# A two-layer MLP behind attention in fp32: the copies of layer one's output leave from another queue, and the order of late conversions changes

## The chip, the core and the metric

The kernel runs on one core of one Trainium2 chip. A core has five engines, each with an instruction queue of its own that is worked off in order: TensorE (matrix products; PE, its weight loads PEld), VectorE (DVE), ScalarE (ACT), GpSimd (POOL) and SyncE (SP), which here only starts DMA transfers. ScalarE can start transfers from its own queue too, in line with its arithmetic. The metric is the device time of one execution in microseconds; of several runs the median counts.

## The reference

Attention over 4 batches, 8 heads, 576 positions and 64 channels gives x, the sum of a local part (each query sees keys less than 4 positions away) and a part on means of 4 positions. Two gated layers follow; the last line is the output, 2304 x 512.

```python
x = np.ascontiguousarray(attn_out.transpose(0, 2, 1, 3)).reshape(B * S, H * D)   # 2304 x 512
h = x @ w_in                                 # layer one, 512 x 2048
x = (h * (1.0 / (1.0 + np.exp(-h)))) @ w_out # 2048 x 512
h = x @ w2_in                                # layer two
out = (h * np.clip(h + 3.0, 0.0, 6.0) / 6.0) @ w2_out
```

## The kernel before

**Numbers.** All products are made from fp32 operands split into a high and a low part of a faster format (hi and lo; `gh`, `gl`, `xhl`, `xa`, `xb`, `w`). Three products, hi by hi, lo by hi and hi by lo, are summed in PSUM. The weights arrive as words of twice the width, so each tile of a weight is converted once: `conv_parts` makes two halves of the number (`wu` on ScalarE, `wt` on GpSimd), `conv_join` puts them together in two operations on VectorE, `split_w` makes hi on ScalarE and lo on GpSimd. One conversion so costs two operations on each of the three.

**Layer one** goes over 8 units of 288 tokens, and in each unit over 16 tiles f of the inner width. For each f: 12 matmuls make h (`gemm1`), ScalarE takes the tanh (`t<-h`), VectorE makes the gate, ScalarE and VectorE or GpSimd split it (`gh`, `gl`), and two f later 12 matmuls add to the four accumulators y (`y_unit1`). The attention of the next unit is woven into these steps. At the end of a unit `end_unit1` (line 965) copies the four y out of PSUM on ScalarE (`yo`) and sends each copy to DRAM (`x2d`), 144 KB a piece; line 969 starts the transfer on ScalarE's queue. Units 0 to 2 are handled in passes of their own; from unit 2 to unit 6 the steps are held in program order (`strict`). Some weights of layer one don't stay in SBUF from unit 2 on: they lie ready in DRAM (`wsd`) and are loaded again each time by `swap_w` (`w<-wsd`), because their slots are used to prepare layer two.

**Preparing layer two.** The first product of layer two is made with seven instead of eight block products, on sums of quarter blocks of `w2_in` and of x. From unit 2 on the sums of the weights are made in small steps (`COMBO`), and `combo_store` (line 292) writes them to DRAM (`wcd`). `load_ring` (line 328) brings them back, 512 KB for each of three parts and 256 KB for the seventh, into 16 slots that layer one's weights free. In the last unit (7), `load_w` loads the 16 tiles of `w2_out` (`raw`, 512 KB each), each as soon as the layer-one tile in its slot is done with; `add_w` (line 1066) lists the 16 conversions, and `step()` runs one after each f from 7 on. `load_x2` loads the first 512 tokens of layer one's output, `sums_x2`, `split_x2a` and `split_x2b` make the sums of x.

**Layer two** goes over 4 blocks of 512 tokens and one of 256, each in 8 steps (`at`, 40 in all). A step makes the seven products (24 matmuls in `first_phase`, 18 in `second_phase`), the gate (`gates2`) and its split into g (two halves, `split_g2`), and adds the two products of the step before (`y_unit2`, 12 matmuls each). Step `at` uses the tiles p and p + 8 of `w2_out`, p counting 0 to 7 in the block.

**Order of the work.** The program text is written in the order in which the steps are meant to go, but a scheduler that simulates the timeline chooses the order of each engine's queue; `tc.issue_after` (in `behind`, `in_line`) pins an instruction behind another. Every transfer reports its end in one of eight counters, named DMAHW0 to DMAHW7 in the listings below; they are given out in turn to the transfers of both queues, and a transfer is started only when the one before it on its counter has ended.

## Time and profile before

| | us |
|---|---|
| median of 3 runs (948.66, 954.82, 953.62) | 953.62 |
| the profiled execution | 943.39 |
| its span, first to last instruction | 941.6 |
| TensorE busy in it | 907.6 |
| VectorE, ScalarE, GpSimd busy | 528.3, 414.1, 354.5 |

The profiled execution is 10.2 us (1.1%) below the median of the runs; 1.8 us of it lie outside the span. TensorE is busy in 96% of the span, so what is left to gain sits in the other 34 us, or in stretches where it runs at the lower of its two clock levels.

### The profile page before, as it was taken

The numbers are of one execution on the slowest core, as the hardware profiler recorded it, in microseconds if no ns is written. First come the engines' busy times: TensorE is split into PE (matmuls) and PEld (weight loads), VectorE is DVE, ScalarE is ACT, GpSimd is POOL, SyncE is SP. The second block draws the span as 40 slices with busy tenths as digits, with TensorE's granted clock in tenths as the row PEclk, the third lists the DMA queues.
The fourth block names the chain that finished last, engine by engine and source line by source line (L and its number), as shares of the span: only waits on it lengthen the run. The fifth ranks groups of instructions, "written<-read, shape, count | busy, mean of one in ns | idle before, by whom it ended". The sixth has DMA issues, their size and how long they took to land.

```text
span 941.6 us, 21071 instructions
## 1 busy us (share of the span) xinstructions
PE 907.6 (96%) x8231; PEld 836.0 (89%) x8231; DVE 528.3 (56%) x1050; ACT 414.1 (44%) x973; POOL 354.5 (38%) x456
## 2 busy tenths in 40 slices
PE   7889989999999799999999989999999999999998
PEld 5778988999999799999999978898888888898896
DVE  4977697266465356654634765556446544644422
ACT  5667546344353354453535443443235324422432
POOL 7568864225554244663345932142006002300100
PEclk9879999999999999999999989999999999999999
DMA  8949846226857648666469985558567655754570
GB/s 209 305 141 282 255 122 153 79 72 163 253 167 200 171 143 202 213 179 203 145 195 350 400 311 176 183 173 267 167 181 227 210 176 171 246 170 153 157 268 24
DMA packets 172908, 185.09 MB, mean 197 GB/s; under 512 B 90632, under 2 KB 140040, under 8 KB 172808
## 3 DMA queue, kind: packets, MB, share of 16 engines
q1 hardware_dynamic: 168200, 179.02, 62.5%
q10 hardware_dynamic: 4608, 4.72, 1.5%
q8 instruction: 65, 1.06, 0.5%
q14 instruction: 35, 0.29, 0.1%
HBM read 154.21 MB, written 29.49 MB: 195 GB/s over the span
## 4 chain that ended last, share of the span: by engine, by line
PE 75%; DMA 7%; DVE 6%; POOL 5%; ACT 3%; issue 3%; SPq 1%; ACTq 0%; DVEq 0%; POOLq 0%
PE y L348 36%; PE m L348 18%; PE h L348 16%; DMA vraw<-in_v_dram 2%; PE lv L348 1%; DVE wt L31 1%; POOL w L31 1%; DMA raw<-in_moe_w_out_dram 1%; POOL wt L31 1%; PE ls L348 1%; DVE t L31 1%; DMA raw<-in_moe_w_in_dram 1%; PE dv L348 1%; DMA qkraw<-in_q_dram 1%; PE dt L355 1%
## 5 line engine op out<-in xcount | busy, mean ns | idle before, releaser
L348 PE MATMUL y<-gh,w 128*128 128x288 f32 x1024 | 230.4, 301 | 12.3 <-ACT gh L31 6.2
L348 PE MATMUL h<-xhl,w 128*128 128x288 f32 x1536 | 232.7, 300 | 4.2 <-DVE t L31 2.4
L348 PEld LDWEIGHTS h<-xhl,w 128*128 128x128 f32 x1536 | 213.0, 191 | 10.9 <-DVE t L31 3.3
L348 PE MATMUL y<-w,g 128*128 128x512 f32 x864 | 216.2, 397 | 2.4 <-ACT g L31 1.2
L348 PEld LDWEIGHTS y<-w,g 128*128 128x128 f32 x864 | 157.0, 188 | 36.8 <-DVE g L31 2.8
L348 PEld LDWEIGHTS y<-gh,w 128*128 128x128 f32 x1024 | 173.6, 191 | 15.8 <-ACT gh L31 7.3
L31 DVE SCALAR_TENSOR_TENSOR t<-t,h 128x288 f32<-128x288 f32 (+1 forms) x192 | 100.7, 527 | 129.6 <-ACT t L31 129.3
L31 POOL TENSOR_TENSOR gl<-t,gh 128x288 fp32r<-128x288 f32 x112 | 94.6, 845 | 175.4 <-ACT gh L31 163.7
L348 PE MATMUL y<-gl,w 128*128 128x288 f32 x512 | 151.0, 300 | 0.7 <-DVE gl L31 0.6
L31 ACT CAST gh<-t 128x288 fp32r<-128x288 f32 x128 | 55.3, 432 | 102.3 <-PE y L348 55.1
L348 PEld LDWEIGHTS y<-gl,w 128*128 128x128 f32 x512 | 97.8, 191 | 2.4 <-DVE gl L31 1.7
L348 PEld LDWEIGHTS m<-xa,ring 128*128 128x128 f32 x720 | 91.8, 191 | 3.4
L348 PE MATMUL m<-xa,ring 128*128 128x256 f32 x720 | 93.4, 282 | 0.0
L31 POOL TENSOR_TENSOR w<-wt,w 128x512 fp32r<-128x512 f32 x48 | 63.2, 1320 | 71.5 <-ACT w L31 64.1
L31 ACT ACTIVATE t<-h 128x288 f32<-128x288 f32 x128 | 52.2, 408 | 85.4 <-PE h L348 73.6
L31 ACT ACTIVATE t<-m,three 128x256 f32<-128x256 f32 x48 | 22.8, 474 | 145.4 <-PE m L348 141.9
L31 DVE SCALAR_TENSOR_TENSOR t<-t,m 128x256 f32<-128x256 f32 x48 | 20.2, 421 | 115.3 <-ACT t L31 115.3
L348 PEld LDWEIGHTS m<-xb,ring 128*128 128x128 f32 x624 | 78.4, 188 | 3.4
L348 PE MATMUL m<-xb,ring 128*128 128x256 f32 x624 | 79.4, 279 | 0.0
L31 DVE SCALAR_TENSOR_TENSOR wt<-wu,wt 128x512 uint32<-128x512 uint32 x96 | 65.4, 685 | 18.7 <-POOL wt L31 11.4
L31 POOL TENSOR_TENSOR xa<-xsum,xa 128x512 fp32r<-128x512 f32 x9 | 12.4, 1385 | 139.4 <-ACT xa L31 139.4
L31 DVE TENSOR_TENSOR g<-t,g 128x512 fp32r<-128x512 f32 (+1 forms) x80 | 59.3, 748 | 9.7 <-ACT g L31 9.6
(94 smaller groups left out, 1056.2 us busy)
## 6 DMA issues: line engine op xcount, KB each, us to landing
ring<-wcd SPq DMA_DIRECT2D x120, 512.0 KB
w<-wsd SPq DMA_DIRECT2D x44, 512.0 KB
raw<-in_moe_w_out_dram SPq DMA_DIRECT2D x32, 512.0 KB
raw<-in_moe_w_in_dram SPq DMA_DIRECT2D x16, 512.0 KB
craw<-in_moe_w_in_dram SPq DMA_DIRECT2D x32, 256.0 KB
sevenths<-wcd SPq DMA_DIRECT2D x32, 256.0 KB
wcd<-chi SPq DMA_DIRECT2D x16, 384.0 KB
wcd<-comb SPq DMA_DIRECT2D x16, 384.0 KB
```

The costliest lines, as they stand in the source:

```text
L31: r = getattr(self.engine, name)(*args, **kwargs)
L348: latest[0] = nc.tensor.matmul(*args, **kwargs).ins
L355: latest[0] = nc.tensor.transpose(*args).ins
```

## The change

Five edits, in the order of the diff. `combo_store` writes one block of sums with two transfers instead of four, because `wcd` gets another layout: for each partition 4 rows of 896 words. `load_ring` then gathers four pieces of 1 KB per partition where it read one of 4 KB, and four of 512 B for the seventh where it read one of 2 KB. The copies of layer one's output (`x2d`) are started from SyncE's queue instead of ScalarE's. In the last unit the third group of ring tiles is no longer written into its program, and seven steps of conversion run instead of nine, in another order of the tiles; in the first block of layer two every step runs two, pinned behind what each engine was last given. And the sums of the next x are pinned in the same way.

```diff
@@ -104,7 +104,7 @@
     x0d = dpool.tile([P, NC, UT], F32, name="x0d")
     y0d = dpool.tile([NC, P, UT], F32, name="y0d")
     wsd = dpool.tile([2, NF, P, 2 * DM], U32, name="wsd")
-    wcd = dpool.tile([HP, P, 3584], U32, name="wcd")
+    wcd = dpool.tile([HP, P, 4, 896], U32, name="wcd")
 
     def setup():
         make_identity(nc, ident)
@@ -292,14 +292,7 @@
     def combo_store(i):
         j, ci = divmod(i, 2)
         for s, t in enumerate((cw["hi", i], cw["c", i])):
-            t = t.bitcast(U32)
-            at = s * 512 + ci * 256
-            nc.sync.dma_start(
-                wcd[j, :, 0:3072].rearrange("p (i w) -> p i w", i=3)[:, :, at:at + 256],
-                t[:, 0:6].rearrange("p (i k) f -> p i (k f)", k=2),
-            )
-            at = 3072 + s * 256 + ci * 128
-            nc.sync.dma_start(wcd[j, :, at:at + P], t[:, 6])
+            nc.sync.dma_start(wcd[j, :, 2 * s + ci], t.bitcast(U32)[:, 0:7].rearrange("p k f -> p (k f)"))
 
 
 
@@ -330,12 +323,14 @@
         src = wcd[q % HP]
         if i < 3:
             t = slot(0, RING[k][i], [P, 2, 2, 2, P], F32R, "ring")
-            nc.sync.dma_start(t.rearrange("p s c k f -> p (s c k f)").bitcast(U32), src[:, i * 1024:(i + 1) * 1024])
+            nc.sync.dma_start(
+                t.rearrange("p s c k f -> p (s c) (k f)").bitcast(U32), src[:, :, 256 * i:256 * (i + 1)]
+            )
         else:
             if k // 2 not in sevenths:
                 sevenths[k // 2] = slot(0, SEVENTHS[k // 2], [P, 2, 2, 2, 1, P], F32R, "sevenths")
             t = sevenths[k // 2][:, k % 2]
-            nc.sync.dma_start(t.rearrange("p s c k f -> p (s c k f)").bitcast(U32), src[:, 3072:3584])
+            nc.sync.dma_start(t.rearrange("p s c k f -> p (s c) (k f)").bitcast(U32), src[:, :, 768:896])
         ring[q, i] = t
 
     def combo(q, n):
@@ -966,7 +961,7 @@
         for m in range(NC):
             yo = pool.tile([P, UT], F32, tag="de" if m == 3 else "le" if u >= NU - 2 else "wt", name="yo", bufs=3)
             act.activation(yo, ys[m], AF.Copy, scale=0.5)
-            nc.scalar.dma_start(x2d[m, :, u * UT:(u + 1) * UT], yo)
+            nc.sync.dma_start(x2d[m, :, u * UT:(u + 1) * UT], yo)
 
     def end_half1(u, ys):
 
@@ -985,7 +980,7 @@
     def end_half2(u, ys):
         for m, yo in enumerate(y0s):
             vec.scalar_tensor_tensor(out=yo, in0=ys[m], scalar=0.5, in1=yo, op0=ALU.mult, op1=ALU.add)
-            nc.scalar.dma_start(x2d[m, :, u * UT:(u + 1) * UT], yo)
+            nc.sync.dma_start(x2d[m, :, u * UT:(u + 1) * UT], yo)
 
     def y_unit2(i, f, ys):
         step_until((1, 1, f))
@@ -1030,10 +1025,10 @@
 
 
     RINGED = {}
-    for n in range(3):
+    for n in range(2):
         for i in range(4):
             f = RING[n][i] if i < 3 else SEVENTHS[n // 2] if n % 2 == 0 else max(RING[n])
-            RINGED.setdefault(15 if n == 2 else f, []).append((n, i))
+            RINGED.setdefault(f, []).append((n, i))
 
     HF = NF // 2
     passes = [(0, range(HF)), (1, range(NF)), (0, range(HF, NF))] + [(u, range(NF)) for u in range(2, NU)]
@@ -1063,7 +1058,7 @@
             if n_pass < 2:
                 step_until((0, 0, f))
             if f == 3 and u == NU - 1:
-                add_w([(1, 1, i) for i in range(NF)])
+                add_w([(1, 1, i) for i in (0, 1, 2, 8, 3, 9, 10, 11, 4, 12, 5, 13, 6, 14, 7, 15)])
             strict[0] = n_pass > 2 and u < NU - 1
             with line():
                 h = gemm1(0, f, x, UT)
@@ -1126,7 +1121,7 @@
                     split_x2a(0)
                 if f == 12:
                     split_x2b(0)
-                if f >= 7:
+                if f >= 9:
                     step()
 
     strict[0] = False
@@ -1213,11 +1208,14 @@
             with in_line():
                 flush(0)
             load_w(1, 1, NF - 1)
-            for i in range(4):
-                load_ring(3, i)
+            for k4 in (2, 3):
+                for i in range(4):
+                    load_ring(k4, i)
             second_phase(u, 1, *first_two[0])
         if u == 0:
-            step()
+            for _ in range(2):
+                with behind(dict(last)):
+                    step()
         for i in (1, 0, 3, 2):
             if at + 4 < n_q and (i < 3 or at + 4 < n_q - HP):
                 load_ring(at + 4, i)
@@ -1232,7 +1230,8 @@
             if p < sizes[u + 1] // XC:
                 load_x2(u + 1, p)
             if p == 4:
-                sums_x2(u + 1)
+                with behind(dict(last)):
+                    sums_x2(u + 1)
         late = p, y2
     for i in range(2):
         y_unit2(i, late[0] + HP * i, late[1])
```

**At the end of a unit.** ScalarE's queue at the end of unit 3, before; `[waits ...]` names the counters of transfers (DMAHW) and of engines for which a row waits.

```order
L31 CAST gh<-t 128x288 [waits DVE_49]
L31 ACTIVATE t<-h 128x288 [waits PE_49,Pool_49]
L31 ACTIVATE yo<-y 128x288 [waits PE_49] x2
L969 DMA x2d<-yo 128x288 [waits DMAHW2_49,Activation_49]
L31 CAST gh<-t 128x288 [waits DVE_49,PE_49]
L969 DMA x2d<-yo 128x288 [waits DMAHW4_49,Activation_49]
L31 ACTIVATE yo<-y 128x288 x2
L31 ACTIVATE t<-h 128x288 [waits PE_49,Pool_49]
L969 DMA x2d<-yo 128x288 [waits DMAHW5_49,Activation_49]
```

SyncE's queue before, a little ahead of that in the program; its fourth row is a reload with the counter DMAHW2, for which the first copy above waits.

```order
L228 DMA w<-wsd 128x1024 [waits DMAHW7_49,PE_49]
L361 DMA qkraw<-in_k_dram 32x18x32 [waits DMAHW0_49]
L361 DMA qkraw<-in_k_dram 32x18x32 [waits DMAHW1_49]
L228 DMA w<-wsd 128x1024 [waits DMAHW2_49,PE_49]
L361 DMA qkraw<-in_q_dram 32x9x32 [waits DMAHW3_49,DVE_49]
L361 DMA qkraw<-in_q_dram 32x9x32 [waits DMAHW4_49]
```

The same place of ScalarE's queue in the changed kernel:

```order
L31 ACTIVATE t<-h 128x288 [waits PE_49,Pool_49]
L31 CAST gh<-t 128x288 [waits DVE_49]
L31 ACTIVATE t<-h 128x288 [waits PE_49,Pool_49]
L31 ACTIVATE yo<-y 128x288 [waits PE_49] x3
L31 CAST gh<-t 128x288 [waits DVE_49,PE_49]
L31 ACTIVATE yo<-y 128x288
L31 ACTIVATE t<-h 128x288 [waits PE_49,Pool_49]
L31 CAST gh<-t 128x288 [waits DVE_49,PE_49]
```

And SyncE's queue there, changed kernel: the four copies stand behind the loads of q and k, and ahead of the stores of sums and four reloads of weights.

```order
L228 DMA w<-wsd 128x1024
L356 DMA qkraw<-in_k_dram 32x18x32 x2
L228 DMA w<-wsd 128x1024
L356 DMA qkraw<-in_q_dram 32x9x32 x4
L356 DMA qkraw<-in_k_dram 32x18x32 x4
L964 DMA x2d<-yo 128x288 x4
L295 DMA wcd<-chi 128x896
L295 DMA wcd<-comb 128x896
L242 DMA craw<-in_moe_w_in_dram 128x2x256 x2
L228 DMA w<-wsd 128x1024 x4
```

What moved: no transfer is left between the tanh, the copies and the split on ScalarE; the copies' transfers stand on SyncE's queue in one piece.

**At the end of layer one.** ScalarE's queue before, from the tanh of f = 12 to the split of f = 14. The rows `t_7999`, `t_8050`, `t_8093` and `t_8144` are the tanh of f = 12, 13, 14 and 15; `wu_8074`, `wu_8117` and `wu_8180` are the first halves of the conversions of tiles 6, 7 and 8.

```order
L31 ACTIVATE t_7999<-h_7986 128x288 [waits PE_49]
L31 CAST gh_8002<-t_7999 128x288 [waits DVE_49,PE_49]
L31 ACTIVATE t_8050<-h_8037 128x288 [waits PE_49,Activation_49]
L31 CAST gh_8053<-t_8050 128x288 [waits DVE_49,PE_49]
L31 ACTIVATE wu_8074<-raw_7827 128x512 [waits DMAHW5_49]
L31 ACTIVATE wu_8117<-raw_7872 128x512 [waits DMAHW1_49]
L31 CAST w_8114<-wt_8076 128x512 [waits DVE_49,DMAHW2_49,Activation_49,Pool_49]
L31 ACTIVATE wu_8180<-raw_7921 128x512 [waits DMAHW4_49]
L31 ACTIVATE t_8093<-h_8080 128x288 [waits PE_49]
L31 CAST w_8177<-wt_8119 128x512 [waits DVE_49,Activation_49,Pool_49]
L31 ACTIVATE t_8144<-h_8123 128x288 [waits PE_49]
L31 CAST gh_8096<-t_8093 128x288 [waits DVE_49]
```

The changed kernel, from the split of f = 12 to the tanh of f = 15. Here `t_8000`, `t_8043` and `t_8086` are the tanh of f = 13, 14 and 15, and `wu_7981`, `wu_8024`, `wu_8067` belong to tiles 8, 3 and 9.

```order
L31 CAST gh_7952<-t_7949 128x288 [waits DVE_49,PE_49]
L31 ACTIVATE wu_7981<-raw_7871 128x512 [waits DMAHW3_49]
L31 ACTIVATE wu_8024<-raw_7676 128x512 [waits DMAHW5_49]
L31 CAST w_8021<-wt_7983 128x512 [waits DVE_49,Activation_49,Pool_49]
L31 ACTIVATE wu_8067<-raw_7925 128x512 [waits DMAHW5_49]
L31 ACTIVATE t_8000<-h_7987 128x288 [waits PE_49]
L31 CAST w_8064<-wt_8026 128x512 [waits DVE_49,Activation_49,Pool_49]
L31 ACTIVATE t_8043<-h_8030 128x288 [waits PE_49]
L31 CAST gh_8003<-t_8000 128x288 [waits DVE_49]
L31 CAST w_8119<-wt_8069 128x512 [waits DVE_49,Activation_49,Pool_49]
L31 CAST gh_8046<-t_8043 128x288 [waits DVE_49]
L31 ACTIVATE t_8086<-h_8073 128x288 [waits DVE_49,PE_49]
```

What moved: the three waits for transfers stood between the tanh of f = 13 and that of f = 14, and stand now between the split of f = 12 and the tanh of f = 13.

**In the first steps of layer two.** VectorE's queue in the step of the third pair, before, from the gate to the next copy from PSUM (`t2` and `h` are the gate, `g2` the two halves of g, `wt` the joining of a converted tile):

```order
L31 SCALAR_TENSOR_TENSOR t2_8187<-t2_8187,m_8409 128x256 [waits Activation_49]
L31 TENSOR_TENSOR h_8436<-m_8410,s_8435 128x512 [waits PE_49]
L31 SCALAR_TENSOR_TENSOR t2_8187<-t2_8187,h_8436 128x256 [waits Activation_49]
L31 SCALAR_TENSOR_TENSOR t2_8187<-t2_8187,h_8436 128x512 [waits Activation_49]
L31 SCALAR_TENSOR_TENSOR wt_8586<-wu_8584,wt_8586 128x512 [waits Activation_49,Pool_49]
L31 TENSOR_TENSOR g2_8186<-t2_8187,g2_8186 128x512 [waits Activation_49]
L31 SCALAR_TENSOR_TENSOR wt_8586<-wu_8584,wt_8586 128x512 [waits DVE_49]
L31 TENSOR_TENSOR g2_8186<-t2_8187,g2_8186 128x512 [waits Activation_49]
L31 TENSOR_TENSOR s_8536<-m_8510,s_8536 128x256 [waits Activation_49]
```

The same step in the changed kernel:

```order
L31 SCALAR_TENSOR_TENSOR t2_8129<-t2_8129,m_8377 128x256 [waits Activation_49]
L31 TENSOR_TENSOR h_8404<-m_8378,s_8403 128x512 [waits PE_49]
L31 SCALAR_TENSOR_TENSOR t2_8129<-t2_8129,h_8404 128x256 [waits Activation_49]
L31 SCALAR_TENSOR_TENSOR t2_8129<-t2_8129,h_8404 128x512 [waits Activation_49]
L31 SCALAR_TENSOR_TENSOR wt_8453<-wu_8451,wt_8453 128x512 [waits Activation_49,Pool_49]
L31 SCALAR_TENSOR_TENSOR wt_8453<-wu_8451,wt_8453 128x512 [waits DVE_49]
L31 SCALAR_TENSOR_TENSOR wt_8462<-wu_8460,wt_8462 128x512 [waits Activation_49,Pool_49]
L31 TENSOR_TENSOR g2_8128<-t2_8129,g2_8128 128x512 [waits Activation_49] x2
L31 TENSOR_TENSOR s_8513<-m_8487,s_8513 128x256 [waits Activation_49]
L31 SCALAR_TENSOR_TENSOR wt_8462<-wu_8460,wt_8462 128x512 [waits DVE_49]
```

What moved: both operations of one conversion and the first of a second one now stand ahead of the two halves of g, where one operation stood ahead of each.

## Rows read from the trace of the kernel before

**Rows 1.** The page: the span, busy time of each engine, granted clock in 40 slices
```profile
span 941.6 us, 21071 instructions
...
PE 907.6 (96%) x8231; PEld 836.0 (89%) x8231; DVE 528.3 (56%) x1050; ACT 414.1 (44%) x973; POOL 354.5 (38%) x456
...
PEclk9879999999999999999999989999999999999999
```

**Rows 2.** The chain of waits, whole run: start us, length us, what
```profile
301.27 3.18 PE y L348 x24
...
309.61 5.40 DMA w<-wsd
...
368.85 3.19 PE y L348 x24
...
429.29 3.18 PE y L348 x24
```

**Rows 3.** Timeline, 300 to 320 us: start, length, engine, line, operation [idle <-releaser]
```profile
308.32 0.71 ACT L31 ACTIVATE yo<-y 128x288 f32<-128x288 f32 x2 [0.19 <-PE y L348]
...
309.61 0.44 SPq L228 DMA_DIRECT2D w<-wsd  x1
...
315.08 0.33 ACTq L969 DMA_DIRECT2D x2d<-yo  x1
315.51 0.43 ACT L31 CAST gh<-t 128x288 fp32r<-128x288 f32 x1 [6.48 <-DMA w<-wsd]
...
316.63 0.58 PE L348 MATMUL y<-gh,w 128*128 128x288 f32 x1 [5.03 <-ACT yo L31]
```

**Rows 4.** Windows of 10 us: PE, PEld, DVE, ACT, POOL busy; clock, DMA share, GB/s
```profile
310.00:320.00 10.00, 4.97 (x27) 4.73 (x26) 0.46 (x1) 3.00 (x7) 3.45 (x7) 0.83 0.91 204
...
540.00:550.00 10.00, 7.38 (x41) 6.83 (x40) 6.85 (x10) 4.39 (x10) 7.71 (x9) 0.77 0.98 386
550.00:560.00 10.00, 10.00 (x77) 10.00 (x77) 4.48 (x10) 3.00 (x8) 0.00 (x0) 0.89 0.80 252
560.00:570.00 10.00, 8.19 (x44) 6.63 (x43) 9.42 (x14) 6.70 (x14) 4.72 (x4) 1.00 0.82 290
...
590.00:600.00 10.00, 10.00 (x65) 8.99 (x65) 5.43 (x11) 3.57 (x8) 1.30 (x1) 1.00 0.56 173
...
640.00:650.00 10.00, 10.00 (x64) 8.84 (x63) 6.63 (x9) 4.89 (x10) 4.54 (x3) 1.00 0.90 299
```

**Rows 5.** Timeline of SyncE's DMA issues, last unit of layer one
```profile
523.45 0.37 SPq L1012 DMA_DIRECT2D x2raw<-x2d  x1
...
527.82 1.58 SPq L157 DMA_DIRECT2D raw<-in_moe_w_out_dram  x2
530.41 0.33 SPq L333 DMA_DIRECT2D ring<-wcd  x1
531.90 0.33 SPq L157 DMA_DIRECT2D raw<-in_moe_w_out_dram  x1
...
536.04 4.21 SPq L157 DMA_DIRECT2D raw<-in_moe_w_out_dram  x4
```

**Rows 6.** Timeline of ScalarE, end of layer one
```profile
539.54 1.18 ACT L31 ACTIVATE wu<-raw 128x512 f32<-128x512 f32 x2 [1.73 <-DMA raw<-in_moe_w_out_dram]
...
543.60 0.39 ACT L31 ACTIVATE t<-h 128x288 f32<-128x288 f32 x1
```

**Rows 7.** Timeline of TensorE, end of layer one
```profile
539.73 3.33 PE L348 MATMUL h<-xhl,w 128*128 128x288 f32 x24
545.68 1.33 PE L348 MATMUL y<-gh,w 128*128 128x288 f32 x4 [2.62 <-ACT gh L31]
```

**Rows 8.** Timeline of VectorE, third column pair of layer two
```profile
580.32 0.68 DVE L31 SCALAR_TENSOR_TENSOR wt<-wu,wt 128x512 uint32<-128x512 uint32 x1
580.92 0.68 DVE L31 TENSOR_TENSOR g<-t,g 128x512 fp32r<-128x512 f32 x1
```

**Rows 9.** Timeline of TensorE, same stretch
```profile
583.26 2.95 PE L348 MATMUL y<-w,g 128*128 128x512 f32 x12
```


## The prediction, made before the changed kernel had run

> **What bounds the kernel now.** I read the page first: TensorE is busy in 907.6 of 941.6 us, and the granted clock leaves its full level in three places, at the start, and in the slices near 310 and 550 us [rows 1]. So the other engines matter only where they make TensorE wait. The chain of waits shows where: between equal marks at the ends of units 2, 3, 4 and 5 lie 67.58 us (301.27 to 368.85) and 60.44 us (368.85 to 429.29); the long unit holds the chain's only transfer in layer one's steady part, a reload of a weight, 5.40 us [rows 2]. The timeline there tells the rest [rows 3]: two copies of y are made at 308.32; the copy's transfer waits in ScalarE's queue for its counter, DMAHW2, whose transfer before it is that reload, started only at 309.61; it is started at 315.08, and the split that stands behind it in the queue begins at 315.51 after 6.48 us of idling. TensorE idled 5.03 us, its window shows a clock of 0.83 [rows 4]. The second place is the end of layer one (540 to 560 us, clock 0.77 and 0.89, DMA share 0.98 [rows 4]): ScalarE waits 1.73 us for a tile of `w2_out`, runs two conversions, and the tanh of f = 14 comes at 543.60 [rows 6]; TensorE, done with h of f = 15 at 543.06 (539.73 + 3.33), waits 2.62 us [rows 7].
>
> **Basis.** The profiled execution took 943.39 us, the median of the runs is 953.62. I make the sum of differences on the profiled execution and set it against the median. What the other 10.2 us are the trace can't show.
>
> **Copies on SyncE's queue.** The waits for counters stay, but now hold up SyncE alone. Behind the copies there stand two stores, two loads for the sums and four reloads; these reloads are for tiles that their unit needs many steps on. At unit 3 the whole stall goes: 67.58 - 60.44 = 7.14 us [rows 2], which holds the idle 5.03 and what the lower clock cost behind it. No other unit end of the trace has one, so the term is **-7.1**. Its bounds are -7.1 and 0: nothing, if the split is then late for another reason; I take the full value, since the row names only the transfer as releaser. For the issues themselves ScalarE gets back 0.33 us each [rows 3], off the path. The rule against this is in the Trainium skill, "DMA: Bandwidth & Descriptors", section "Issuing engines are not separate DMA queues": transfers of all queues run on the same 16 engines, and another issuing engine saves only the time of issuing. The row disagrees as far as the wait stood in ScalarE's queue itself and held its arithmetic for 6.48 us. By the rule alone this term would be about nothing, a rival below.
>
> **The end of layer one.** What the path waits for is a tile's landing. SyncE's issues show the pace of a full queue: each follows the landing of the transfer eight before it. Tiles in 4 KB pieces follow each other at (4.21 - 0.33) / 3 = 1.29 us; where the one that landed was `x2raw`, in 1 KB pieces and of the same 512 KB, it is 531.90 - 530.41 = 1.49 us [rows 5]. So a ring transfer in 1 KB pieces costs an estimated 0.20 us more. The tile that released ScalarE at 539.54 is tile 6; tile 9 was issued after one ring more and lands two spacings later, at 539.54 + 2 x 1.29 = 542.1. In the changed order one ring and one tile fewer stand ahead of tile 9 (-2.6), five rings cost 0.2 more each (+1.0), and two stores instead of four an estimated 0.4 less: tile 9 at about 540.1. Its conversion on ScalarE (0.59, half of 1.18 [rows 6]) and the tanh of f = 13 (0.39) follow, then a VectorE step of the gate of the same size, and h of f = 15, which needs the PSUM buffer of f = 13, can start at 541.5, where TensorE is free from about 539.7: an idle 1.8 us instead of 2.62. Then 12 matmuls of h (half of 3.33 [rows 7]) and 24 of y (3.18 [rows 2]) lead to layer two at 546.3. Before, y of f = 14 began at 545.68, 4 of its 12 matmuls took 1.33 at the low clock [rows 7], which puts the same point at about 549.1 (545.68 + 2.5 x 1.33). That is 2.8 us; with 0.11 x 10 us of clock lost in 550 to 560 [rows 4] and regained, I take **-3.7**. Bounds: with the tile soon enough for no wait at all, 1.8 us less idling and so -5.5; with tile 9 where it was (542.1), h of f = 15 starts at 543.5, TensorE idles 3.8, the 36 matmuls run in part at the clock that rows 7 show, and the point comes at about 550.8, +1.7. I take the earlier landing because the count of transfers ahead is exact, and only their spacing is estimated. The same page has a table "Specifications" by which pieces from 512 B up move at line rate; by it the rings cost nothing more, and this term would be about 1.0 better. Rows 5 show 0.20 for 1 KB pieces.
>
> **The first steps of layer two.** Seven conversions instead of nine are done before, so the first block makes nine in five steps where it made seven in seven. A further conversion is 2 x 0.68 on VectorE [rows 8], two of 0.6 on ScalarE, and two on GpSimd, which has work in 1.30 of 10 us in such a window [rows 4]. From 560 to 570 VectorE is busy 9.42 of 10 and TensorE only 8.19 [rows 4]: there 1.36 us of VectorE's work is on the path, less one operation of 0.68 that no longer stands ahead of the first g: **+0.7**. In the later steps one `wt` more and 1.2 us of ScalarE's work stand ahead of g; g ends at 581.60 and its products start at 583.26, so 1.66 us cover both [rows 8, 9], and the cost is 0. If that cover is gone, because a conversion there waits for its tile with g behind it, each of four steps loses up to 1 us: bounds -0.7 and +4.
>
> **The rest** is 0. The sums of the next x run on GpSimd, which is nearly empty there [rows 4]. The ring's slower pieces in layer two lie beside TensorE, which is 100% busy at a DMA share of 0.56 [rows 4]; 0.20 of 1.29 makes that an estimated 0.65. The stores halve in number on a queue that hides them.
>
> **Sum:** -7.1 - 3.7 + 0.7 = -10.1, so 943.39 becomes 933.3, and the median 953.62 becomes **943.5**. About 1%, 9.5 us, is what a measurement of this kernel can tell from no change; the forecast lies just beyond.
>
> **Rivals.** First, a conversion's wait takes the stall's place at the end of layer one: the waits for tiles now stand ahead of the tanh of f = 13, one step earlier than before, and if the landings don't move, the term is +1.7: -7.1 + 1.7 + 0.7 = -4.7, 948.9. For it speaks the DMA share of 0.98 [rows 4]; against it the shorter count of transfers. Chance 0.24. Second, the stall at unit 3 stays, because something else is late there: -3.0, 950.6. Against it: the split's only releaser is the reload [rows 3], chance 0.04; the skill's rule above would give this time. Third, the runs' 10.2 us above the profiled execution hold a stall of the same kind at another unit's end, which goes too: 7.1 more, 936.4. For it: where the counters fall is the same in each run, but how late a reload lands depends on its run; against it, the profiled execution has just one. Chance 0.17. Fourth, on the slow side: the ring in 1 KB pieces becomes the bound of layer two. Some 120 transfers cost 0.20 us more each, 24 us; on the path this stands only where DMA engines are full. The windows show 0.56 in the middle of a block and 0.90 at a block's start [rows 4], so it decides only if the pieces cost far more than the row says. Then 24 - 10.1 = +13.9, 967.5. Chance 0.05. The forecast keeps 0.50.
>
> **From cases to chances.** Two thirds of the forecast's 0.50 fall beyond -1%, and nearly all of the third rival's 0.17: faster 0.49. The other third, the first and the second rival are within 1%: 0.46. The fourth is slower: 0.05. The range goes from the third rival, 936, to the second, 951; outside lie the fourth and the tails.
>
> **What the changed profile would show.** Unit 3 takes about 60 us like its neighbours, ScalarE's queue has no transfer, and SyncE shows the waits for counters instead. The idle time ahead of the last h and y in layer one is under 2.6 us, and layer two begins some 3 us earlier counted from the unit's start. Rings follow each other at 1.5 us in a full queue. Products y in steps 1 to 4 of layer two don't wait for g. I am wrong if a split or a tanh of layer one still waits long behind something on ScalarE, if a reload behind the copies on SyncE is late for its matmul, or if layer two's matmuls wait for rings.

## The result, and the profile after

The changed kernel took 939.54 us (median of four runs, 937.39 to 940.60), the kernel before 951.14 beside it (948.08 to 954.82). The ratio is 0.9874 with a 95% interval of 0.9827 to 0.9921: 1.3% faster. Forecast were 943.5, with a range of 936 to 951.

The page of the changed kernel shows hardly a difference to [rows 1]; the span is only 3.8 us shorter, against 11.6 us between the medians. That gap is itself a finding, to which the experiments come back.

```profile
span 937.8 us, 21033 instructions
...
PE 904.7 (96%) x8231; PEld 832.5 (89%) x8231; DVE 529.1 (56%) x1050; ACT 413.6 (44%) x973; POOL 353.5 (38%) x456
...
PEclk9889999999999999999999989999999999999999
```

The chain of waits has the same marks, at the ends of units 3, 4 and 5:

```profile
302.30 3.18 PE y L343 x24
...
363.90 3.18 PE y L343 x24
...
425.28 3.18 PE y L343 x24
```

From 302.30 to 363.90 are 61.60 us where [rows 2] had 67.58, and the reload is no longer in the chain. The timeline of ScalarE at that place:

```profile
309.35 1.01 ACT L31 ACTIVATE yo<-y 128x288 f32<-128x288 f32 x3 [0.19 <-PE y L343]
310.28 0.43 ACT L31 CAST gh<-t 128x288 fp32r<-128x288 f32 x1
```

The split follows the three copies at once, where it had waited 6.48 us [rows 3]. The wait is now SyncE's: its timeline has the four copies' transfers 10 us after the first copy was made. No matmul waits for them in this profile:

```profile
319.31 2.16 SPq L964 DMA_DIRECT2D x2d<-yo  x4
```

A smaller wait is left in this pass. TensorE stands for 1.57 us (0.70 before) ahead of the last product of the attention's local scores `ls`, and the profile doesn't tell for what:

```profile
320.25 0.19 PE L343 MATMUL ls<-xe 64*32 64x32 f32 x1 [1.57 <-issue]
```

At the end of layer one a wait has stayed. ScalarE, from the split of f = 12 to the tanh of f = 14:

```profile
528.27 0.44 ACT L31 CAST gh<-t 128x288 fp32r<-128x288 f32 x1 [1.11 <-PE y L343]
534.00 1.18 ACT L31 ACTIVATE wu<-raw 128x512 f32<-128x512 f32 x2 [5.29 <-DMA raw<-in_moe_w_out_dram]
536.92 0.62 ACT L31 CAST w<-wt 128x512 fp32r<-128x512 f32 x1 [1.75 <-DVE wt L31]
537.45 0.63 ACT L31 ACTIVATE wu<-raw 128x512 f32<-128x512 f32 x1
538.02 0.39 ACT L31 ACTIVATE t<-h 128x288 f32<-128x288 f32 x1
538.31 0.61 ACT L31 CAST w<-wt 128x512 fp32r<-128x512 f32 x1
538.82 0.41 ACT L31 ACTIVATE t<-h 128x288 f32<-128x288 f32 x1
```

VectorE there, four joins in a row:

```profile
534.80 2.62 DVE L31 SCALAR_TENSOR_TENSOR wt<-wu,wt 128x512 uint32<-128x512 uint32 x4 [5.60 <-POOL wt L31]
```

And TensorE:

```profile
531.23 3.33 PE L343 MATMUL h<-xhl,w 128*128 128x288 f32 x24
537.47 3.25 PE L343 MATMUL h<-xhl,w 128*128 128x288 f32 x12 [2.90 <-DVE wt L31]
540.51 0.77 PE L343 MATMUL y<-gh,w 128*128 128x288 f32 x4
```

ScalarE stands for 5.29 us on the load of tile 8, three times the 1.73 that it stood for tile 6 before [rows 6]; the tanh of f = 13 comes at 538.02, behind work on three conversions. TensorE idles 2.90 us (2.62 [rows 7]), and the 12 matmuls of h behind it take 3.25 us, as long as the 24 of the row above. The windows (columns as in [rows 4]) show the clock:

```profile
530.00:540.00 10.00, 7.10 (x45) 6.87 (x44) 4.40 (x8) 3.98 (x9) 4.25 (x5) 0.86 1.09 364
540.00:550.00 10.00, 10.00 (x81) 10.00 (x81) 6.09 (x12) 3.02 (x7) 3.80 (x5) 0.97 1.05 386
550.00:560.00 10.00, 7.79 (x50) 6.91 (x50) 7.28 (x12) 7.00 (x15) 3.67 (x4) 0.89 1.10 352
```

So the clock still falls at the wait, to 0.86 where the window with the wait had 0.77 [rows 4]. The 0.89 of the last window is another place. Before, it came from the first products m of layer two, still slow behind the wait, and the first products y of layer two ran at the full clock:

```profile
549.06 3.71 PE L348 MATMUL m<-xa,ring 128*128 128x256 f32 x18
...
562.89 0.50 PE L348 MATMUL y<-w,g 128*128 128x512 f32 x1 [0.78 <-ACT g L31]
564.42 5.63 PE L348 MATMUL y<-w,g 128*128 128x512 f32 x23 [1.03 <-DVE g L31]
```

In the changed kernel these m run at the full clock, and the y behind the first g are slow (granted clock 0.62 from 557 to 560 us):

```profile
543.75 2.27 PE L343 MATMUL m<-xa,ring 128*128 128x256 f32 x18
...
556.66 0.50 PE L343 MATMUL y<-w,g 128*128 128x512 f32 x1 [1.35 <-ACT g L31]
558.01 7.03 PE L343 MATMUL y<-w,g 128*128 128x512 f32 x23 [0.86 <-DVE g L31]
```

### The profile page after: what moved, and what is told of

Read it like the earlier page. It is cut to its first block, busy times and chain, and to the rows that moved or that the text cites. A ratio compares the mean times of both kernels' runs of the same rounds, so it can differ in the third digit from the quotient of the medians.

```text
span 937.8 us, 21033 instructions
## 1 busy us (share of the span) xinstructions
PE 904.7 (96%) x8231; PEld 832.5 (89%) x8231; DVE 529.1 (56%) x1050; ACT 413.6 (44%) x973; POOL 353.5 (38%) x456
## 4 chain that ended last, share of the span: by engine, by line
PE 81%; DVE 7%; DMA 4%; POOL 3%; ACT 2%; issue 2%; SPq 1%; DVEq 0%; POOLq 0%; ACTq 0%
PE y L343 39%; PE h L343 18%; PE m L343 18%; PE lv L343 1%; DVE wt L31 1%; DVE t L31 1%; DMA raw<-in_moe_w_out_dram 1%; PE ls L343 1%; DMA vraw<-in_v_dram 1%; PE dv L343 1%; DMA nat<-in_q_dram 1%; POOL w L31 1%; POOL wt L31 1%; PE ds L343 1%; PE dt L350 1%
## 5 line engine op out<-in xcount | busy, mean ns | idle before, releaser
L343 PE MATMUL y<-gh,w 128*128 128x288 f32 x1024 | 227.5, 299 | 4.8 <-ACT gh L31 3.8
L343 PEld LDWEIGHTS y<-gh,w 128*128 128x128 f32 x1024 | 171.7, 189 | 8.0 <-ACT gh L31 4.4
L31 DVE TENSOR_TENSOR g<-t,g 128x512 fp32r<-128x512 f32 (+1 forms) x80 | 60.3, 760 | 10.1 <-ACT g L31 9.7
```

The costliest lines, as they stand in the source:

```text
L31: r = getattr(self.engine, name)(*args, **kwargs)
L343: latest[0] = nc.tensor.matmul(*args, **kwargs).ins
```

## The experiments

Each profile was cut into stages by the start times of matmuls, in the order of the timeline: the first h of a unit's pass, or the first product m of layer two. "Prologue" runs from the middle of unit 1's pass to the start of unit 2's; "end of unit 3" is the pass of unit 4, at whose start the copies of unit 3 are made (the texts written ahead call this stage unit 3); "end of layer one" runs from the middle of unit 7's pass to the first m; "start of layer two" is the first six of its 40 steps, and "rest" what follows to the end of the span. Ratios are to the kernel before, with 95% intervals.

| kernel | prologue | end of unit 3 | end of layer one | start of layer two | rest | ratio |
|---|---|---|---|---|---|---|
| before, first profile | 70.00 | 67.58 | 33.06 | 62.96 | 329.58 | |
| before, again | 72.61 | 68.44 | 34.22 | 64.03 | 329.45 | 0.9998 (0.9968 to 1.0027) |
| changed | 71.31 | 61.59 | 31.79 | 63.84 | 330.23 | 0.9874 (0.9827 to 0.9921) |
| changed, again | 71.27 | 61.15 | 32.29 | 63.98 | 330.30 | 0.9907 (0.9889 to 0.9925) |
| copies alone | 77.60 | 60.71 | 39.99 | 61.42 | 329.51 | 0.9965 (0.9936 to 0.9995) |
| all but the copies | 70.93 | 70.69 | 31.93 | 63.62 | 330.56 | 0.9979 (0.9951 to 1.0007) |
| orders alone | 70.16 | 68.93 | 32.18 | 63.61 | 330.36 | 1.0003 (0.9972 to 1.0034) |
| copies and orders | 71.13 | 60.39 | 30.82 | 64.01 | 329.61 | 0.9888 (0.9854 to 0.9922) |
| copies and layout | 74.52 | 60.47 | 40.83 | 62.58 | 330.16 | 1.0037 (1.0010 to 1.0063) |
| copies, tile 6 last | 77.88 | 61.02 | 29.64 | 62.91 | 329.46 | 0.9874 (0.9850 to 0.9899) |
| changed, ring group early (what ran is the changed kernel) | 72.82 | 63.36 | 31.17 | 63.84 | 330.23 | 0.9915 (0.9881 to 0.9949) |
| changed, five conversions | 70.37 | 60.99 | 28.25 | 64.21 | 330.32 | 0.9863 (0.9838 to 0.9888) |
| the same, again | 77.44 | 61.01 | 27.81 | 64.18 | 329.89 | 0.9875 (0.9825 to 0.9925) |
| five conversions, old layout | 70.74 | 60.96 | 27.33 | 64.20 | 329.63 | 0.9877 (0.9845 to 0.9910) |

### The copies alone

```diff
-            nc.scalar.dma_start(x2d[m, :, u * UT:(u + 1) * UT], yo)
+            nc.sync.dma_start(x2d[m, :, u * UT:(u + 1) * UT], yo)
```

(in the kernel before, at both places.)

> The kernel before with one edit, the copies of layer one's output started from SyncE's queue. Theory A (the gain is the waits for counters taken off ScalarE's queue): 8 to 12 us faster than before in the timed runs, and in its profile unit 3 takes about 60.5 us. Theory B (most of the gain comes from the order of the last unit's conversions and from layer two): 0 to 4 us faster. Theory C (a reload or another load behind the copies on SyncE is now late): within 2 us of before, with a new wait of TensorE at a unit's end.

It took 947.60 us against 949.85. The stall went as theory A had it (60.71), but the end of layer one took 39.99 us. ScalarE there:

```profile
537.98 0.44 ACT L31 CAST gh<-t 128x288 fp32r<-128x288 f32 x1 [1.11 <-PE y L348]
547.46 1.18 ACT L31 ACTIVATE wu<-raw 128x512 f32<-128x512 f32 x2 [9.05 <-DMA raw<-in_moe_w_out_dram]
550.37 0.62 ACT L31 CAST w<-wt 128x512 fp32r<-128x512 f32 x1 [1.72 <-DMA ring<-wcd]
550.89 0.62 ACT L31 ACTIVATE wu<-raw 128x512 f32<-128x512 f32 x1
551.45 0.40 ACT L31 ACTIVATE t<-h 128x288 f32<-128x288 f32 x1
```

TensorE's row behind it:

```profile
553.18 1.33 PE L348 MATMUL y<-gh,w 128*128 128x288 f32 x4 [8.90 <-ACT gh L31]
```

A wait of 9.05 us for a tile took the place of the one removed, at another place, and TensorE idled 8.90. Theory A's mechanism held, but its time didn't. The time, 2.25 us faster, lies in theory B's range, but not for B's reason: the stall's 7 us were won and lost again elsewhere. Theory C came nearest: it missed its "within 2 us" by little, and a load that is late with a new wait of TensorE at a unit's end is what the rows show. Why that load is late comes below.

### All but the copies

The changed kernel with the diff above reversed.

> The changed kernel with the copies started from ScalarE's queue again. Theory A: 0 to 3 us faster than before, and its profile shows one or more waits of several us in ScalarE's queue behind a copy's transfer. Theory B: 6 us or more faster than before. If the counters shift so that no copy meets a late transfer, A and B can't be told apart by the time, and the profile decides.

947.85 us, 2.0 us faster, is in theory A's range. ScalarE's timeline at the end of unit 3:

```profile
320.70 0.43 ACT L31 CAST gh<-t 128x288 fp32r<-128x288 f32 x1 [8.42 <-DMA qkraw<-in_q_dram]
```

The releaser is here a load of q, of another counter than DMAHW2, and the wait is longer than 6.48 us [rows 3]. So the stall was no accident of one counter and one reload: with either counter, the transfer that had it before stood late in SyncE's full queue.

### The kernel before, again

No edit.

> The kernel before, unchanged, for a second profile and for the spread of its runs. Ratio 1.00. Theory D (the timed runs above the first profiled one hold more or longer stalls of the same kind): the profile shows a wait behind a copy's transfer at another unit's end, or a longer one at unit 3's, in proportion to its time above 943.4 us. Rival: the spread lies elsewhere (in the prologue or in a lower granted clock), and units 3 to 6 take 67.6, 60.4, 60.4 and 59.9 us again.

A span of 948.2 us where the first profile had 941.6. The stall is there again and little longer:

```profile
319.85 0.43 ACT L31 CAST gh<-t 128x288 fp32r<-128x288 f32 x1 [7.13 <-DMA w<-wsd]
```

The rest is spread: 2.6 in the prologue, 2.5 in the pass of unit 3 ahead of the stall (59.88 and 62.36, not in the table), 1.2 at the end of layer one, 1.1 at the start of layer two, and 1.6 less ahead of the prologue's stage. Theory D falls for the most part: the stall's stage gives 0.9 of the 6.6. The first profile, on which the prediction was made, was a quick execution (943.39 us; the quickest of 35 later ones took 943.77); between the second profiles (948.2 and 938.5) lie 9.7 us, near to what the medians say.

### The orders alone

```diff
-    for n in range(3):
+    for n in range(2):
...
-                add_w([(1, 1, i) for i in range(NF)])
+                add_w([(1, 1, i) for i in (0, 1, 2, 8, 3, 9, 10, 11, 4, 12, 5, 13, 6, 14, 7, 15)])
...
-                if f >= 7:
+                if f >= 9:
...
-            step()
+            for _ in range(2):
+                with behind(dict(last)):
+                    step()
```

(and the ring group after f = 15 moved to layer two, the sums pinned.)

> The kernel before with only the edits to order: ring groups, list and number of conversions, two pinned conversions per step in layer two's first block, pinned sums. My prediction: -3.7 at the end of layer one and +0.7 at the start of layer two, so 3 us faster than before. Rival from the changed kernel's trace, where the time from the middle of unit 7 to layer two fell by 1.3 us and 1.0 was given back in layer two: within 1 us of before.

Ratio 1.0003. The end of layer one is 0.9 to 2.0 us shorter than in the two profiles of before, the last column gives 0.8 back, and the time shows no difference: the rival's case. So 0.3% from the copies and 0.0% from the orders stand against 1.3% from the whole. The parts need each other, and the next two runs say which.

### Copies with one other part each

The diff of the copies, with the order edits, and with the new layout of `wcd`.

> Copies on SyncE's queue and the edits to order, with the old layout of the sums in DRAM. In the profile of the copies alone, unit 3 was 7 us shorter and the end of layer one (middle of unit 7 to layer two) 40.0 us instead of 33.1 and 34.2. Theory F (the edits to order give that back: fewer conversions wait and the third ring group is out of unit 7): end of layer one at about 32 us, 9 to 12 us faster than before. Rival G (the layout with two stores instead of four gives it back): end of layer one near 38 to 40 us, 2 to 4 us faster than before.

> Copies on SyncE's queue and the new layout (two stores instead of four, ring gathered in 1 KB pieces), with the old order of the last unit and of layer two. Theory F: end of layer one stays near 38 to 41 us, 2 to 4 us faster than before. Rival G: end of layer one about 32 to 34 us, 8 to 11 us faster than before. Either way units 3 to 6 as in the changed kernel (unit 3 about 61 us).

With the orders 938.18 us against 948.91, with the layout 951.65, and the end of layer one 30.82 and 40.83 us. That is theory F: the orders give back what the copies lose there, the layout doesn't. The second kernel's whole time missed F's "2 to 4 us faster": it is 0.37% slower than before, where the copies alone were 0.35% faster, and the two intervals don't overlap. Its profile can't tell why, because the profiled execution (947.66 us) is the quickest of its twelve; the cause stays open.

### One tile

Why the copies lose 6 us at a place where SyncE's queue has only gained four small transfers is to be seen in the order of that queue. The scheduler had reordered the loads. The tiles of `w2_out`, as SyncE loads them:

```
before:       0 1 2 3 5 4 7 8 6 9 10 11 12 13 14 15
copies alone: 0 1 2 5 3 4 7 8 9 10 11 6 12 13 14 15
```

Tile 5 went one place forward, and tile 6 from the 9th place to the 12th (issued 6 us after the 9th), while its conversion stayed ahead of those of tiles 7 and 8 and of the tanh of f = 14 in ScalarE's queue. The list of the changed kernel begins with 0, 1, 2, 8, 3, 9, 10: the conversion of tile 6 is thirteenth, in layer two, and does no harm. The test leaves SyncE's queue as it was with the copies alone and moves tile 6 in the list:

```diff
-                add_w([(1, 1, i) for i in range(NF)])
+                add_w([(1, 1, i) for i in (0, 1, 2, 3, 4, 5, 7, 8, 9, 10, 11, 12, 13, 14, 15, 6)])
```

> The kernel before with the copies on SyncE's queue, and the list of conversions with tile 6 at its end; SyncE's queue is the same as with the copies alone, where the load of tile 6 had moved from the 9th to the 12th place among the tiles of w2_out while its conversion stayed the first of the last three in layer one. Theory J (this one late tile is the 6 us that the copies alone lose): the end of layer one falls from 40.0 to 32 to 35 us, 6 to 9 us faster than before. Rival K (SyncE's queue as a whole runs late, by its stores that wait for sums): it stays at 38 to 40 us, 2 to 4 us faster than before.

Theory J: 938.34 us against 949.50, and 29.64 us at the end of layer one, both better than expected. ScalarE there:

```profile
540.23 0.63 ACT L31 ACTIVATE wu<-raw 128x512 f32<-128x512 f32 x1
542.89 0.62 ACT L31 CAST w<-wt 128x512 fp32r<-128x512 f32 x1 [2.04 <-DVE wt L31]
543.42 0.62 ACT L31 ACTIVATE wu<-raw 128x512 f32<-128x512 f32 x1
544.65 0.41 ACT L31 ACTIVATE t<-h 128x288 f32<-128x288 f32 x1 [0.61 <-PE h L348]
```

No conversion waits for a load there. With the same order of loads, the place of one conversion decides over the loss. Two edits, the queue of the copies and the place of one tile in the list, gain as much as the whole change.

### The ring group written early

```diff
-    for n in range(2):
+    for n in range(3):
...
-            RINGED.setdefault(f, []).append((n, i))
+            RINGED.setdefault(15 if n == 2 else f, []).append((n, i))
```

(in the changed kernel, and the group taken out of layer two again.)

> The changed kernel with the third group of ring tiles written into the last unit again, after f = 15. My prediction counted one ring less ahead of tile 9, and so with it: tile 9 lands some 1.5 us later and the end of layer one grows by up to 1.5 us, 0 to 1.5 us slower than the changed kernel. Rival: the ring group is what fills the queue there, and the end of layer one grows by 4 us or more.

The edit changed the text of the program and not what ran: as far as the traces tell, SyncE, ScalarE, VectorE and GpSimd have the same instructions in the same order as in the changed kernel, the 669 transfers of SyncE with the same counters. So this is a third profile of the changed kernel. It tests neither the prediction's term for one ring less ahead of tile 9 nor the rival, and it shows that this part of the change had no effect of its own beside the others.

What it gives is the spread: 943.33 us against 948.91, ratio 0.9915, with 63.36 us at the end of unit 3 and 31.17 at the end of layer one, where the other two profiles have 61.59 and 61.15, 31.79 and 32.29.

### Five conversions instead of seven

```diff
-                if f >= 9:
+                if f >= 11:
```

(in the changed kernel.)

> The changed kernel with five conversions in the last unit instead of seven (steps after f = 11 to 15), two more in layer two's first block. In the changed kernel's profile ScalarE waits 5.29 us for a tile ahead of the tanh of f = 13, and TensorE 2.90 us. Theory H (this wait is what the end of layer one still loses): middle of unit 7 to layer two falls from 31.8 to 28 to 30 us, the first steps of layer two give back at most 1.5, in sum 1 to 3 us faster than the changed kernel (936.5 to 938.5). Rival I (the tile's landing sets the end wherever the conversion stands, ahead of f = 15 now, or the conversions are too many for layer two): within 1 us of the changed kernel or slower.

> The changed kernel with five conversions in the last unit, once more, because its ratio to before (0.9863, interval 0.9838 to 0.9888) and that of the changed kernel's repeat (0.9907, 0.9889 to 0.9925) only just part. If the gain over the changed kernel is real: ratio 0.984 to 0.988 again, and the end of layer one at 27.3 to 28.5 us against 31.8 and 32.3. If it was the chip of that job: 0.989 to 0.992.

> Copies on SyncE's queue, the edits to order with five conversions in the last unit instead of seven, and the old layout of the sums in DRAM: the parts that the runs so far showed to pay, without the new layout. If the layout is worth nothing: the same as the changed kernel with five conversions (935.8). If the ring's smaller pieces cost time at the end of layer one or in layer two: 1 to 2 us faster than that (934 to 935). If the two stores instead of four save more than the pieces cost: 1 us or more slower (937 or above).

Theory H holds for the place: 28.25 and 27.81 us, and the start of layer two gives back 0.2 to 0.4 us. ScalarE at the end of layer one of the first of these runs:

```profile
532.44 0.41 ACT L31 ACTIVATE t<-h 128x288 f32<-128x288 f32 x1 [1.22 <-PE h L343]
533.98 0.44 ACT L31 CAST gh<-t 128x288 fp32r<-128x288 f32 x1 [1.13 <-PE y L343]
534.32 1.19 ACT L31 ACTIVATE wu<-raw 128x512 f32<-128x512 f32 x2
537.05 0.62 ACT L31 CAST w<-wt 128x512 fp32r<-128x512 f32 x1 [1.54 <-DVE wt L31]
538.72 0.41 ACT L31 ACTIVATE t<-h 128x288 f32<-128x288 f32 x1 [1.06 <-PE h L343]
```

The tanh of f = 14 and its split (the first two rows) run in step with TensorE; two conversions stand ahead of the tanh of f = 15 alone, their tiles are there, and TensorE doesn't wait at all between the middle of unit 7 and layer two. For the whole time the medians are 935.78, 938.88 and 937.49 us, the ratios 0.9863, 0.9875 and 0.9877. The changed kernel has 0.9874, 0.9907 and, with the run above, 0.9915; the intervals overlap. So 3 to 4.5 us are shown in the stage; a gain in the whole is likely and not settled. The run with the old layout was to tell what the layout is worth beside five conversions: its time lies in the third case written ahead (937 or above), its ratio can't be told from the other two.

**The changed kernel again.**

> The changed kernel once more, beside the others on the same chip, for a second profile: ratio to before 0.985 to 0.990. If the spread of its profiles is that of the kernel before, its prologue differs by 1 to 3 us from 71.3 for the pass of unit 1; units 3 to 6 and the end of layer one within 1 us of 61.6, 145.0 and 31.8.

941.00 us, ratio 0.9907, just outside the range expected; the prologue, expected to differ by 1 to 3 us, is the same to 0.1 us. The other stages are as expected.

## Why the prediction was right, and where not

**The stall: right.** Forecast -7.1. Against the two profiles of before (67.58, 68.44) the three of the changed kernel (61.59, 61.15, 63.36) are 4.2 to 7.3 us shorter, and in all ten profiles with copies on SyncE the stage takes 60.4 to 63.4 us, in the four with copies on ScalarE 67.6 to 70.7. What is missing from the full 7.1 is the smaller wait ahead of `ls`: in nine of the ten it is 0.36 to 1.57 us, and the stage without it is 60.0 us each time; in the tenth, with 63.36, it is 1.90 us and the granted clock falls behind it (0.83 from 317 to 327 us). The second rival (the stall stays because something else is late) is out, and with it the result that the Trainium skill ("DMA: Bandwidth & Descriptors", section "Issuing engines are not separate DMA queues") would give, that another issuing engine saves only the time of issuing. Here the time was in the wait of the issuing engine, 6.48 to 8.42 us in three profiles, and taking the issue off that engine saved it. What the forecast didn't see is how the gain hangs on the rest: by itself this edit was worth 0.3%, because the order of the loads and that of their conversions no longer went together.

**The end of layer one: mis-sized.** The forecast of -3.7 was made of -2.8 up to layer two's first product and -0.9 for the clock regained behind it. The first part measured -1.3 between the first profiles (33.06 to 31.79) and -1.9 between the second. The places came as worked out: the middle of unit 7 is 4.03 us earlier than before, so the forecast for h of f = 15, 541.5, is 537.47 in the changed kernel's time, and its row begins at 537.47. Tile 9 came nearly as counted: GpSimd, which waits for its load, begins with it at 536.92, which is 540.95 in the time of before, against 540.1 in the forecast and 542.1 in the first rival. That the row of h fits exactly is luck. The forecast let h of f = 15 wait for the tanh of f = 13, but that tanh begins at 538.02, after h; the profile names VectorE's joins of tiles 8 and 3, which the forecast left out, and TensorE, there earlier, idled 2.90 us instead of 1.8. What failed is the next step, "then 12 matmuls of h (half of 3.33) and 24 of y": the first 12 took 3.25 us at the fallen clock instead of 1.67. The outcome of this part lies between the forecast and the first rival: a conversion's wait did take the stall's place, and without it, with five conversions, the stage is another 3 to 4.5 us shorter. The second part came, in full: the first 18 products m took 3.71 us before (3.31 in the repeat) and 2.27 in the changed kernel.

**Layer two's start: right in sum, with luck.** Forecast +0.7. The stage says +0.9 between the first profiles and 0.0 between the second; but the regained clock, 1.4 and 1.05 us, lies in this stage too, so the rest of it cost 2.3 and 1.0 us. One piece is steady: the third to sixth step together take 42.7 us with the edits to order (42.9 to 43.0 with five conversions) and 42.1 without, in all fourteen profiles. That is 0.6 us, where the forecast had nothing, and TensorE shows no idle time there; where it comes from isn't shown. The forecast's own place, the first products y, changes by the clock: the 23 of them take 5.63 us in the first profile of before and 7.18 in the repeat, 7.0 to 7.2 in every profile with the edits to order. The first wait for g there grew from 0.78 to 1.35 us between the first profiles.

**The rest, forecast 0: wrong by about 0.7 us.** Of the seven profiles with the old layout six have 329.5 to 329.6 us in the last column, and one, the orders alone, 330.36; of the seven with the new layout six have 330.2 to 330.6 and one 329.89. At the end of layer one the layout goes with 0.3 to 1.5 us more in three comparisons (28.25 and 27.81 against 27.33; 31.79, 32.29 and 31.17 against 30.82; 40.83 against 39.99) and 0.25 less in the fourth (31.93 against 32.18). So the new layout likely costs 1 to 2 us in the profiles, and nothing shows that fewer stores gave anything. By whole runs it cost 7 us beside the copies alone (ratios 1.0037 and 0.9965) and nothing clear of noise beside the edits to order. The forecast's 0.20 us for a ring in small pieces rests on one spacing of 1.49 us against a mean of three that lie between 0.98 and 1.58 us in the same trace, so [rows 5] don't show it. What the traces do show is that SyncE is busy longer with issuing one such ring, 0.52 us instead of 0.32 (medians of 120).

**The basis.** The third rival put the 10.2 us of runs above the profile down to one more stall. The repeat, 6.6 us longer, shows otherwise: they are spread over the prologue and several stages, and the stall has 0.9 of them.

The forecast of -10.1 us on the profiled execution was in truth -3.8 there, because that execution was quick; on the medians it was -11.6, and -8.5 and -5.6 in the two later measurements of the changed kernel (the second is the run with the ring group early). The direction and the main term were right; that the sum came out so near has luck in it.

## What to carry to other kernels

Here a transfer that was started from ScalarE's queue held ScalarE's arithmetic until its counter was free (6.48, 7.13 and 8.42 us in three profiles), and the transfer that had the counter before was a late one of another queue; look for an engine that idles on a DMA which isn't its own. After moving transfers between queues, compare the order of all loads on the receiving queue with the order in which their users stand: one load that a scheduler moved three places ate most of the gain here, and one number in a list brought it back. See whether an edit to the program's text changed any engine's queue at all: one of the tests here didn't. Take two profiles of the kernel before, and cut both into stages, before a sum is made against one of them.

## What the runs showed of the hardware

The same program differs by 7 us in one stage between two executions. The five conversions and their repeat are one program. In the prologue VectorE works on `vd` as loads of v land; its rows in the first, for the last three of these loads:

```profile
133.96 2.07 DVE L31 TENSOR_REDUCE vd<-vraw 72x128 f32<-72x512 f32 x2
...
137.51 1.06 DVE L31 TENSOR_REDUCE vd<-vraw 72x128 f32<-72x512 f32 x1 [0.88 <-DMA vraw<-in_v_dram]
```

Those of the second:

```profile
135.43 2.07 DVE L31 TENSOR_REDUCE vd<-vraw 72x128 f32<-72x512 f32 x2 [1.07 <-DMA vraw<-in_v_dram]
...
139.93 1.01 DVE L31 TENSOR_REDUCE vd<-vraw 72x128 f32<-72x512 f32 x1 [1.83 <-DMA vraw<-in_v_dram]
```

The chain of waits has the last of the loads with 2.42 us in the first and 3.37 in the second. TensorE, which waits behind VectorE, in the timeline of the first:

```profile
139.58 1.85 PE L343 MATMUL h<-xhl,w 128*128 128x288 f32 x12 [1.67 <-DVE t L31]
```

And of the second:

```profile
141.96 3.25 PE L343 MATMUL h<-xhl,w 128*128 128x288 f32 x12 [3.71 <-DVE t L31]
```

The windows of the first give the clock as full:

```profile
140.00:150.00 10.00, 9.85 (x68) 8.58 (x67) 10.00 (x26) 6.80 (x20) 4.88 (x5) 1.00 0.63 162
150.00:160.00 10.00, 9.03 (x73) 7.71 (x73) 8.04 (x27) 7.02 (x23) 4.75 (x6) 1.00 0.64 147
```

Those of the second don't:

```profile
140.00:150.00 10.00, 8.04 (x29) 6.75 (x30) 8.79 (x18) 4.16 (x8) 5.03 (x6) 0.55 0.61 158
150.00:160.00 10.00, 10.00 (x56) 9.31 (x56) 6.67 (x24) 3.91 (x15) 0.80 (x1) 0.76 0.37 59
```

VectorE waited 2.0 us longer for loads (0.88 us against 1.07 and 1.83), and so did TensorE (1.67 us against 3.71); behind it the granted clock was 0.55 and 0.76 of full speed, and the same 12 matmuls took 3.25 us instead of 1.85. The stage grew from 70.37 to 77.44 us, 7.1 us for 2.0 us of waiting.

The same wait parts all fourteen profiles. In eight it is 1.5 to 1.7 us, and the prologue takes 70.0 to 71.3 us; in six it is 3.2 to 3.8 us, and the prologue takes 72.6 to 77.9. Three kernels have profiles of both kinds with the same instructions: the kernel before, the changed kernel and the one with five conversions. So it is a matter of the execution and not of an edit. How much is lost behind the wait depends on the clock: in the 20 us around and behind it two windows of 10 us have 0.83 and 1.00 in the profiles of 72.6 and 72.8 us, 0.66 and 1.00 in that of 74.5, about 0.6 and 0.73 in those of 77.4 to 77.9. Why the loads are later in some executions isn't shown. It is one reason why runs of one program spread (943.8 to 955.7 us in 35 runs of the kernel before); that it is the main one isn't shown either.
